# One DMA per raw Q, K, V chunk, and matmuls that read each block of 160 columns as two streams 80 columns apart

## The chip, the cores and the metric

The kernel runs on one core of one Trainium2 chip. The metric is the device time of one execution in microseconds (us). Before the change three runs gave 609.98, 607.99 and 611.25 us; their median is 609.98 us.

The engines of a core as the profile names them: PE multiplies matrices (PEld is its loading of the stationary operand), DVE and ACT work on vectors, POOL is the general engine, and SP here only issues transfers. SBUF is the on-chip memory with 128 partitions, PSUM the memory into which PE adds up its products. A matmul keeps one operand (128 x 128) stationary and streams the other, the moving operand, past it, column by column.

## The reference

With S = 2048 tokens, D = 640, F = 1536, H = 32 heads of 20:

```python
xn  = layernorm(x)
qkv = xn @ wqkv                     # (2048, 640) @ (640, 1920): queries, keys, values
idx = pos[:, None] - arange(8) * 2  # each token looks at 8 tokens, two apart, backwards
s   = softmax(q . k[idx] * scale) @ v[idx] @ wo        # masked where idx < 0
g   = silu(silu(xn @ w1) @ w2)      # (640, 1536), (1536, 640)
out = x + s * g
```

All values are float32.

## The kernel before

**Tiles.** The tokens are worked on in four groups of 512 (`NG = 4`): two halves of the sequence by two parities, since a window takes every second token. A group has `T = 4` tiles of 128 tokens. In each group the phase `qkv_phase` makes the queries, keys and values, then `ffn_phase` makes the two feed-forward products, with the product by `wo` of the group before in between; the last group's `wo` stands at the end (`wo_last`).

**Products in three parts.** Every float32 operand is split into a high part (rounded to the type fp32r) and a low part (the rest). A product is high x high + low x high + high x low: three matmuls (L881, L882, L883 for queries, keys and values, L1060 to L1062 for `w1`, L925 and L927 for `w2` and `wo`).

**The query, key and value phase.** It runs in four quarters (`NQ`), each with 8 heads = `CQ` = 160 columns of Q, of K and of V, 480 together. A quarter adds up over `DC` = 5 chunks of 128 rows of `wqkv`; for each chunk and each of 4 token tiles come three matmuls with the 480 columns as moving operand, so 60 matmuls in a quarter. ACT then copies the sums out of PSUM, K and V together by L633 and Q by L635, and SP moves rows of K and V between partitions (`halo`, L646). DVE makes the scores (L672, L675) and weighs the values (L714, L720).

**Weights.** Each chunk of weights passes through a ring of 7 SBUF tiles (`WR`, printed `w0` to `w6`). At its first use the raw chunk is loaded by `raw_load` (issued at L521) into a place lent by another tile (`pr`, `xr` or `gate`), ACT makes the high part (L557) and DVE or, for the first ten chunks, POOL the low part (L561); the two halves are then stored to memory (L566) and later loaded again by POOL (L548). Of Q, K and V 20 chunks are split, 8 of them twice, so `raw_load` brings 28 such chunks.

**Order of columns before.** A raw chunk of 480 columns is brought by two DMAs. It lies in SBUF as two halves of 240 columns: K and the first half of Q, then V and the second half of Q. The helper `two` makes the matmul read column m and column m + 240 in turn, so that in PSUM K and V alternate, and behind them the two halves of Q; `paired` reads every second column when ACT copies.

**Order of the work.** `Weave` records every operation with an assumed duration and an order of priority, plays the whole through and emits the instructions in the order of the starts that it assumes; PE's order is given by the program, the others' come out of that play. A DMA of SP counts with 0.62 us for each transfer of a raw chunk at the start and 0.45 later (`len(pairs)` is the number of transfers), one of ACT with 0.65. `LANES = 8` is the number of transfers of an engine that `Weave` lets be under way. In the first quarter (`first_quarter`, matmuls at L828) PE's order is a list written by hand (`FIRST`), since data are still arriving: the four token tiles of x are loaded one by one (L836, L583), get their statistics (L797, L798) and are normalised (L802), PE transposes them (L812), and ACT and DVE split them (L816, L817).

Of the kernel before, what the change touches and what calls it, by code (L numbers as in the profile page):

```python
# [10 lines left out]
AF = mybir.ActivationFunctionType  # L11
# [4 lines left out]
S, D, F, H, DH = 2048, 640, 1536, 32, 20  # L16
# [4 lines left out]
CQ = HQ * DH  # L21
# [3 lines left out]
HALO = W - 1  # L25
# [45 lines left out]
def two(ap, at, n, apart):  # L71

    a = [list(ap.ap[0]), [1, n // 2], [apart, 2]]
    return bass.AP(tensor=ap.tensor, offset=ap.offset + at, ap=a)


def paired(ps, h=2):

    return ps.rearrange("p (m h) -> p h m", h=h)


def halves_of(ap):
    return ap.rearrange("p (h m) -> p h m", h=2)


def tsl(t):
    return slice(t * P, (t + 1) * P)
# [218 lines left out]
def local_attention_silu_ffn(ctx: ExitStack, tc: tile.TileContext, x, wqkv, wo, w1, w2, out):  # L306
    nc = tc.nc
# [72 lines left out]
    def bank():  # L380
        i = take("acc", 6)
        return ACC[i], ("acc", i)
# [6 lines left out]
    mm = lambda n: n / 2400 + 0.0027  # L389
# [7 lines left out]
    def act(n, fn, reads, writes, prio, table=None, more=0.0, late=0.0, at=0.0, spans=()):  # L397
        return add("ACT", ac(n) + more, fn, reads, writes, prio, table=table, late=late, at=at, spans=spans)
# [64 lines left out]
    for u in units:  # L463
        n = seen[u] = seen.get(u, 0) + 1
# [6 lines left out]
    def width(i):  # L471
        return 3 * CQ if units[i][0] == "q" else D
# [8 lines left out]
    def raw_tile(k):  # L481


        if k < DC:
            return "pr", k
        if k < early:
            s = (k - DC) % 6
            return ("xr", s) if s < 2 else ("g", s - 2)
        return "xr", k % 3

    def raw_load(k):
        i = fresh[k]
# [12 lines left out]
        if u[0] == "q":  # L505
            _, q, c = u
            whole = wqkv[c * P:(c + 1) * P, :]
            to = halves_of(r)
            pairs.append((to[:, :, :CQ], whole[:, D:].rearrange("p (s m) -> p s m", s=2)[:, :, q * CQ:(q + 1) * CQ]))
            pairs.append((to[:, :, CQ:], halves_of(whole[:, q * CQ:(q + 1) * CQ])))  # L510
        elif u[0] == "w1":
            pairs.append((r.rearrange("p (c f) -> p c f", c=DC),
                          w1.rearrange("(c p) f -> p c f", p=P)[:, :, u[1] * P:(u[1] + 1) * P]))
        else:
            m = wo if u[0] == "wo" else w2
            pairs.append((r, m[u[1] * P:(u[1] + 1) * P, :]))
        by = nc.scalar if k in BY_ACT else nc.sync

        def go():
            for to, frm in pairs:  # L520
                by.dma_start(to, frm)  # L521
        if k in BY_ACT:
            add("ACT", 0.65 * len(pairs), go, [], kr, -1, nbytes=n * P * 4)
            return
        dma(go, [], kr, n * P * 4, 1 + k if k < 2 * DC else clock[0] + 5, (0.62 if k < 2 * DC else 0.45) * len(pairs))
# [51 lines left out]
    def w_done(n=1):  # L577
        for _ in range(n):
            w_load()
# [50 lines left out]

    def evac_qkv(g, q, t, ps, kp):
        kv, qq = KV[q], Q[q]
        act(2 * CQ, lambda: nc.scalar.activation(kv[:, :, HALO + t, :], paired(ps[:, :2 * CQ]), AF.Copy),  # L633
            [kp], [(k, q, t) for k in ("kv", "own", "val")], -1 if (g, q) in KEYS_FIRST else 0)
        act(CQ, lambda: nc.scalar.activation(halves_of(qq[:, t, :]), paired(ps[:, 2 * CQ:3 * CQ]), AF.Copy), [kp], [("q", q, t)], 0)  # L635

    def halo(g, q):
        h, par = groups[g]
# [139 lines left out]
    def first_quarter(i):  # L778

        ps, ws = {}, []  # L780
# [39 lines left out]
        def product(t, k, c):  # L820

            o, kp = ps[t]
            x, kx = (TL, "tl") if k == 1 else (TH, "th")
            wh, wl, kh, kl = ws[c]
            w, kw = (wl, kl) if k == 2 else (wh, kh)
            first, last = t not in given, given.get(t, 0) == 3 * DC - 1
            given[t] = given.get(t, 0) + 1
            pe(mm(3 * CQ), lambda: nc.tensor.matmul(  # L828
                o[:, :3 * CQ].rearrange("p (m h) -> p m h", h=2), x[i][:, c, tsl(t)], two(w, 0, 3 * CQ, 3 * CQ // 2),
                start=first, stop=last), [(kx, i, c, t), kw], [kp])  # L830

        given = {}
# [14 lines left out]
        for t in range(T):  # L847
            b, kp = bank()
# [15 lines left out]
    def qkv_phase(g, i, io):  # L864
        for q in range(NQ):
            if g == 0 and q == 0:
                ps = first_quarter(i)
            else:
                ps = [bank() for t in range(T)]
                for c in range(DC):  # L870
                    wh, wl, kh, kl = w_next("q", q, c)
                    for t in range(T):
                        o, kp = ps[t]

                        n = wh.shape[-1]

                        def unit(c=c, t=t, o=o, wh=wh, wl=wl, n=n):
                            o = o[:, :n].rearrange("p (m h) -> p m h", h=2)
                            hi, lo = TH[i][:, c, tsl(t)], TL[i][:, c, tsl(t)]
                            vh, vl = (two(w, 0, n, n // 2) for w in (wh, wl))  # L880
                            nc.tensor.matmul(o, hi, vh, start=c == 0, stop=False)  # L881
                            nc.tensor.matmul(o, lo, vh, start=False, stop=False)  # L882
                            nc.tensor.matmul(o, hi, vl, start=False, stop=c == DC - 1)  # L883
                        pe(3 * mm(n), unit, t_keys(i, [c], [t]) + [kh, kl], [kp])
# [287 lines left out]
```

## Time and profile before

| | before |
|---|---|
| median of three runs | 609.98 us |
| the profiled execution, its own time | 607.58 us |
| its span in the profile | 605.8 us |
| granted PE clock | 0.999 of full speed |
| PE busy, of the span | 596.8 us, 99% |
| DVE, ACT, POOL busy | 519.7, 222.1, 164.1 us |
| mean rate of all DMA | 265 GB/s |

The profile is of one execution. "Busy" of PE overlaps and its ends are modelled, so a matmul's cost is read from the distance between the starts of two that follow each other, in a timeline. A row of a timeline gives start and duration in us, the engine (SPq and ACTq are the queues from which transfers are issued), the line, operation, tile written and tiles read, how often, and in brackets the idle time before it with what ended it. In a table by stages a row gives the stretch, its length, each engine's busy time with the number of its instructions, the granted clock, the mean busy share of the 16 DMA engines and GB/s. The core's transfers by SP are in DMA queue q1.

### The profile page before, as it was taken

The numbers are of one execution on the slowest core, as the hardware profiler recorded it, in microseconds if no ns is written. First come the engines' busy times: TensorE is split into PE (matmuls) and PEld (weight loads), VectorE is DVE, ScalarE is ACT, GpSimd is POOL, SyncE is SP. The second block draws the span as 40 slices with busy tenths as digits, with TensorE's granted clock in tenths as the row PEclk, the third lists the DMA queues.
The fourth block names the chain that finished last, engine by engine and source line by source line (L and its number), as shares of the span: only waits on it lengthen the run. The fifth ranks groups of instructions, "written<-read, shape, count | busy, mean of one in ns | idle before, by whom it ended". The sixth has DMA issues, their size and how long they took to land.

```text
span 605.8 us, 9169 instructions
## 1 busy us (share of the span) xinstructions
PE 596.8 (99%) x3495; PEld 561.1 (93%) x3495; DVE 519.7 (86%) x505; ACT 222.1 (37%) x426; POOL 164.1 (27%) x229
## 2 busy tenths in 40 slices
PE   7999999999999999999999999999999999999997
PEld 6999989999999999999999999999999999999897
DVE  6498999989899998999979998999727999998534
ACT  5436465444535323343325421342512351314220
POOL 5800102233110153343221126533122133431100
PEclk9999999999999999999999999999999999999999
DMA  8999999977999999665699999866789997766742
GB/s 251 315 270 300 299 410 396 352 259 235 283 344 334 338 281 295 196 195 141 192 331 288 335 334 303 257 198 186 219 215 288 306 320 252 253 186 206 212 158 87
DMA packets 70151, 160.81 MB, mean 265 GB/s; under 512 B 13421, under 2 KB 34125, under 8 KB 70109
## 3 DMA queue, kind: packets, MB, share of 16 engines
q0 software_dynamic: 19296, 79.31, 43.5%
q1 hardware_dynamic: 50125, 80.52, 43.2%
q8 instruction: 27, 0.44, 0.3%
q10 hardware_dynamic: 688, 0.41, 0.2%
q14 instruction: 15, 0.12, 0.1%
HBM read 107.91 MB, written 34.16 MB: 235 GB/s over the span
## 4 chain that ended last, share of the span: by engine, by line
PE 91%; DMA 5%; DVE 2%; SPq 1%; issue 0%; ACT 0%; ACTq 0%; DVEq 0%
PE acc L925 22%; PE acc L927 14%; PE acc L881 9%; PE acc L883 9%; PE acc L882 9%; PE rot L1060 8%; PE rot L1062 8%; PE rot L1061 8%; PE rot L612 2%; PE acc L828 1%; DMA half_w<-w 1%; DMA gate<-in_B_w_dram 1%; DMA half_q<-w 1%; DMA pr<-in_A_wqkv_dram 1%; DMA xin<-in_A_x_dram 1%; SPq L521 1%
## 5 line engine op out<-in xcount | busy, mean ns | idle before, releaser
L881 PE MATMUL acc<-w,th 128*128 128x480 f32 x300 | 110.8, 369 | 0.0
L882 PE MATMUL acc<-w,tl 128*128 128x480 f32 x300 | 109.8, 366 | 0.0
L883 PE MATMUL acc<-w,th 128*128 128x480 f32 x300 | 109.8, 366 | 0.0
L925 PE MATMUL acc<-w,sh 128*128 128x384 f32 x384 | 109.1, 330 | 0.0
L672 DVE TENSOR_TENSOR pr<-q,kv 128x2560 f32<-128x2560 f32 x32 | 91.9, 2873 | 19.7 <-DMA kv<-kv 19.4
L927 PE MATMUL acc<-w,sh 128*128 128x256 f32 x384 | 104.7, 273 | 0.0
L1060 PE MATMUL rot<-th,w 128*128 128x512 f32 x240 | 92.3, 385 | 1.5 <-DVE tl L622 1.0
L714 DVE TENSOR_TENSOR pr<-q,kv 128x2560 f32<-128x2560 f32 x32 | 90.3, 2822 | 1.0
L1061 PE MATMUL rot<-tl,w 128*128 128x512 f32 x240 | 91.0, 379 | 0.0
L1062 PE MATMUL rot<-th,w 128*128 128x512 f32 x240 | 91.0, 379 | 0.0
L675 DVE TENSOR_REDUCE l<-pr 128x128 f32<-128x2560 f32 x32 | 89.7, 2802 | 0.3
L548 POOL DMA_DIRECT2D w<-half_w x72 | 38.9, 540 | 161.5 <-PE acc L927 54.0
L927 PEld LDWEIGHTS acc<-w,sh 128*128 128x128 f32 x384 | 73.7, 192 | 0.6
L925 PEld LDWEIGHTS acc<-w,sh 128*128 128x128 f32 x384 | 72.6, 189 | 0.6
L1073 ACT ACTIVATE sh<-rot 128x512 fp32r<-128x512 f32 x48 | 28.7, 598 | 112.8 <-PE rot L1062 112.7
L548 POOL DMA_DIRECT2D w<-half_q x52 | 27.8, 535 | 120.6 <-PE acc L883 71.5
L883 PEld LDWEIGHTS acc<-w,th 128*128 128x128 f32 x300 | 56.7, 189 | 4.0
L882 PEld LDWEIGHTS acc<-w,tl 128*128 128x128 f32 x300 | 56.7, 189 | 3.8
L881 PEld LDWEIGHTS acc<-w,th 128*128 128x128 f32 x300 | 56.7, 189 | 3.8
L925 PE MATMUL acc<-w,sl 128*128 128x384 f32 x192 | 55.9, 328 | 0.0
L1060 PEld LDWEIGHTS rot<-th,w 128*128 128x128 f32 x240 | 45.4, 189 | 7.9 <-DVE tl L622 1.2
L616 ACT ACTIVATE th<-rot 128x512 fp32r<-128x512 f32 x33 | 19.8, 600 | 88.8 <-PE rot L612 88.7
(101 smaller groups left out, 1084.0 us busy)
## 6 DMA issues: line engine op xcount, KB each, us to landing
w<-half_w POOLq DMA_DIRECT2D x72, 640.0 KB, 5.4
w<-half_q POOLq DMA_DIRECT2D x52, 480.0 KB, 4.7
half_w<-w SPq DMA_DIRECT2D x24, 640.0 KB
half_q<-w SPq DMA_DIRECT2D x20, 480.0 KB
kv<-kv SPq DMA_DIRECT2D x15, 560.0 KB
w<-half_wo POOLq DMA_DIRECT2D x10, 640.0 KB, 5.4
kv<-kv SPq DMA_DIRECT2D x15, 420.0 KB
gate<-in_B_w_dram SPq DMA_DIRECT2D x16, 320.0 KB
```

The source lines that it names most:

```text
L548: add("POOL", 1.0, lambda: nc.gpsimd.dma_start(both, src), [("half", u)], [kh, kl], due + 10, nbytes=2 * n * P * 4)
L672: dve(2560, lambda: nc.vector.tensor_tensor(out=PR, in0=win(qq[:, t:t + 2, :], W, 0), in1=win(kv[:, 0, t:t + 2, :], W, CQ), op=OP.mult), h ...
L675: dve(2560, lambda: nc.vector.tensor_reduce(out=l[:, t:t + 2].rearrange("p t w h -> p (t w h)"), in_=PR.rearrange("p t w (h d) -> p (t w h ...
L714: dve(2560, lambda: nc.vector.tensor_tensor(out=PR.rearrange("p t w (h d) -> p t (w h) d", d=DH), in0=e[:, t:t + 2].rearrange("p t w h -> ...
L881: nc.tensor.matmul(o, hi, vh, start=c == 0, stop=False)
L882: nc.tensor.matmul(o, lo, vh, start=False, stop=False)
L883: nc.tensor.matmul(o, hi, vl, start=False, stop=c == DC - 1)
L925: nc.tensor.matmul(a[t][0][:, :CA].rearrange("p (m h) -> p m h", h=2), st, col_a(w), start=first, stop=last)
L927: nc.tensor.matmul(b[t // 2][0][:, h * CB:(h + 1) * CB].rearrange("p (m h) -> p m h", h=2), st, col_b(w), start=first and h == 0, stop=las ...
L1060: nc.tensor.matmul(to, wh[:, cs], hi, start=c == 0, stop=False)
L1061: nc.tensor.matmul(to, wh[:, cs], lo, start=False, stop=False)
L1062: nc.tensor.matmul(to, wl[:, cs], hi, start=False, stop=c == DC - 1)
```

## The change

The raw chunk comes by one DMA of three runs of 160 columns a partition, and lies in SBUF as Q, K, V, in the order of the matrix. The helper `trio` replaces `two` for these chunks: the matmul reads, in each of the three blocks of 160 columns, column m and column m + 80 in turn. `trio_sums` names the same 480 PSUM columns as 3 x 80 x 2, which is one unbroken run as before. The copies out of PSUM (L633 and L635 before) take blocks 1 and 2 and block 0 and put the two halves of a block side by side. Nothing else in the program's text is changed; the ring, the split into high and low, the stored halves and the other matmuls (`two` with 320 and 256 columns between the streams) stay.

```diff
+def trio(w):
+
+    return bass.AP(tensor=w.tensor, offset=w.offset, ap=[list(w.ap[0]), [CQ, 3], [1, CQ // 2], [CQ // 2, 2]])
+
+
+def trio_sums(ps):
+    return ps[:, :3 * CQ].rearrange("p (k m h) -> p k m h", k=3, h=2)
@@ raw_load
-            to = halves_of(r)
-            pairs.append((to[:, :, :CQ], whole[:, D:].rearrange("p (s m) -> p s m", s=2)[:, :, q * CQ:(q + 1) * CQ]))
-            pairs.append((to[:, :, CQ:], halves_of(whole[:, q * CQ:(q + 1) * CQ])))
+            pairs.append((r.rearrange("p (k m) -> p k m", k=3), whole.rearrange("p (k m) -> p k m", k=3)[:, :, q * CQ:(q + 1) * CQ]))
@@ evac_qkv
-        act(2 * CQ, lambda: nc.scalar.activation(kv[:, :, HALO + t, :], paired(ps[:, :2 * CQ]), AF.Copy),
+        sums = trio_sums(ps).rearrange("p k m h -> p k h m")
+        act(2 * CQ, lambda: nc.scalar.activation(kv[:, :, HALO + t, :].rearrange("p k (h m) -> p k h m", h=2), sums[:, 1:], AF.Copy),
...
-        act(CQ, lambda: nc.scalar.activation(halves_of(qq[:, t, :]), paired(ps[:, 2 * CQ:3 * CQ]), AF.Copy), [kp], [("q", q, t)], 0)
+        act(CQ, lambda: nc.scalar.activation(halves_of(qq[:, t, :]), sums[:, 0], AF.Copy), [kp], [("q", q, t)], 0)
@@ product (first quarter)
-                o[:, :3 * CQ].rearrange("p (m h) -> p m h", h=2), x[i][:, c, tsl(t)], two(w, 0, 3 * CQ, 3 * CQ // 2),
+                trio_sums(o), x[i][:, c, tsl(t)], trio(w),
@@ qkv_phase
-                            o = o[:, :n].rearrange("p (m h) -> p m h", h=2)
...
-                            vh, vl = (two(w, 0, n, n // 2) for w in (wh, wl))
+                            vh, vl = trio(wh), trio(wl)
```

Since a chunk now counts as one transfer, `Weave` plays the program through with other durations, and the order of SP, DVE and ACT changes in the first three groups; PE's order is the same. Lines of the changed program stand 7 or 8 lower than before in these places (L521 is L528, L561 is L568).

SP at the very start (`xin` is the tile for x, `pr` and `xr` hold raw chunks), before:

```order
L836 DMA xin_105<-in_A_x_dram 128x320
L583 DMA xin_105<-in_A_x_dram 128x640
L521 DMA pr_102<-in_A_wqkv_dram 128x2x160
L521 DMA pr_102<-in_A_wqkv_dram 128x2x80
L521 DMA pr_102<-in_A_wqkv_dram 128x2x160
L521 DMA pr_102<-in_A_wqkv_dram 128x2x80
L521 DMA pr_102<-in_A_wqkv_dram 128x2x160
L521 DMA pr_102<-in_A_wqkv_dram 128x2x80
L521 DMA pr_102<-in_A_wqkv_dram 128x2x160
L521 DMA pr_102<-in_A_wqkv_dram 128x2x80
L583 DMA xin_105<-in_A_x_dram 128x640
L521 DMA xr0_107<-in_A_wqkv_dram 128x2x160
```

The same place after the change:

```order
L844 DMA xin_105<-in_A_x_dram 128x320
L590 DMA xin_105<-in_A_x_dram 128x640
L528 DMA pr_102<-in_A_wqkv_dram 128x3x160 x4
L590 DMA xin_105<-in_A_x_dram 128x640
L528 DMA xr0_107<-in_A_wqkv_dram 128x3x160
L528 DMA xr1_108<-in_A_wqkv_dram 128x3x160
L590 DMA xin_105<-in_A_x_dram 128x640
```

Eight issues between the second and the third token tile of x became four.

DVE in the first group, where the scores of quarter 0 and the low parts of the chunks of quarters 2 and 3 are made (`w5` and `w6` are the third and fourth chunk of quarter 2, `w0` the fifth, `w1` the first of quarter 3), before:

```order
L672 TENSOR_TENSOR pr_102<-q0_97,kv0_93 128x2560
L561 TENSOR_TENSOR w5_80<-xr1_108,w5_80 128x480
L561 TENSOR_TENSOR w6_81<-gate_106,w6_81 128x480
L561 TENSOR_TENSOR w1_76<-gate_106,w1_76 128x480
L675 TENSOR_REDUCE l0_103<-pr_102 128x128
L561 TENSOR_TENSOR w0_75<-gate_106,w0_75 128x480
```

The same place after the change:

```order
L680 TENSOR_TENSOR pr_102<-q0_97,kv0_93 128x2560
L568 TENSOR_TENSOR w5_80<-xr1_108,w5_80 128x480
L683 TENSOR_REDUCE l0_103<-pr_102 128x128
L568 TENSOR_TENSOR w6_81<-gate_106,w6_81 128x480
L568 TENSOR_TENSOR w0_75<-gate_106,w0_75 128x480
L568 TENSOR_TENSOR w1_76<-gate_106,w1_76 128x480
```

The long reduction of the scores moved ahead of the low part of `w6`.

More of the change, by code (lines that the diff above doesn't have):

```diff
@@ L873, in qkv_phase, with unit @@
                         o, kp = ps[t]
-                        n = wh.shape[-1]
-                        def unit(c=c, t=t, o=o, wh=wh, wl=wl, n=n):
-                            o = o[:, :n].rearrange("p (m h) -> p m h", h=2)
+                        def unit(c=c, t=t, o=trio_sums(o), wh=wh, wl=wl):
                             hi, lo = TH[i][:, c, tsl(t)], TL[i][:, c, tsl(t)]
-                            vh, vl = (two(w, 0, n, n // 2) for w in (wh, wl))
+                            vh, vl = trio(wh), trio(wl)
                             nc.tensor.matmul(o, hi, vh, start=c == 0, stop=False)
@@ L883, in unit @@
                             nc.tensor.matmul(o, hi, vl, start=False, stop=c == DC - 1)
-                        pe(3 * mm(n), unit, t_keys(i, [c], [t]) + [kh, kl], [kp])
+                        pe(3 * mm(3 * CQ), unit, t_keys(i, [c], [t]) + [kh, kl], [kp])
                     w_done()
```

## The prediction

> **What bounds it.** I read the page's busy times and its chain first, then a table by stages, then timelines of the one stage in which PE idles.
>
> ```profile
> PE 596.8 (99%) x3495; PEld 561.1 (93%) x3495; DVE 519.7 (86%) x505; ACT 222.1 (37%) x426; POOL 164.1 (27%) x229
> PE 91%; DMA 5%; DVE 2%; SPq 1%; issue 0%; ACT 0%; ACTq 0%; DVEq 0%
> ...
> 7.39:22.82 15.43, 14.71 (x78) 12.39 (x77) 9.39 (x27) 8.50 (x23) 10.30 (x11) 1.00 1.00 297
> 22.82:59.30 36.48, 36.48 (x182) 34.04 (x181) 30.01 (x35) 17.02 (x38) 7.05 (x6) 1.00 1.00 293
> 59.30:135.00 75.70, 75.21 (x449) 70.03 (x448) 72.52 (x68) 37.98 (x67) 15.18 (x17) 1.00 0.97 340
> 135.00:602.00 467.00, 465.70 (x2766) 440.33 (x2764) 403.69 (x358) 155.69 (x295) 128.25 (x189) 1.00 0.85 252
> ```
>
> PE is busy for 99% of the span, and 91% of the chain that ends last is PE. The stages are the first quarter (from its first product to its last), the other three quarters of group 0, its feed-forward phase, and all the rest. Length less PE's busy time is idle time: 0.72, 0.00, 0.49 and 1.30 us, 2.5 us together. So only two things can move the end by much: the time that a matmul takes, or a new wait of PE. DMA is the second thing to see: its share is 1.00 from 7 to 59 us, so a transfer there waits for bytes ahead of it.
>
> **The matmuls.** The change touches those with 480 columns.
>
> ```profile
> L881 PE MATMUL acc<-w,th 128*128 128x480 f32 x300 | 110.8, 369 | 0.0
> L828 PE MATMUL acc<-w,th 128*128 128x480 f32 x40 | 11.5, 382 | 0.0
> L828 PE MATMUL acc<-w,tl 128*128 128x480 f32 x20 | 6.7, 385 | 0.0
> ...
> 22.82 0.37 PE L881 MATMUL acc<-w,th 128*128 128x480 f32 x1
> 59.27 0.38 PE L1060 MATMUL rot<-th,w 128*128 128x512 f32 x1
> ...
> 104.18 0.38 PE L1062 MATMUL rot<-th,w 128*128 128x512 f32 x1
> 105.91 0.38 PE L1061 MATMUL rot<-tl,w 128*128 128x512 f32 x1
> ```
>
> There are 15 quarters of 60 (L881 to L883, 300 each) and 60 in the first quarter: 960. The 0.37 is a modelled length; the cost is the distance of starts. From 22.82 to 59.27 stand three quarters, 180 matmuls: 36.45 / 180 = 0.2025 us each, 0.422 ns a column, and 960 x 0.2025 = 194.4 us in all. The matmuls for `w1` read their 512 columns as two streams 256 apart: eight starts in 105.91 - 104.18 = 1.73 us are 0.216 each, again 0.422 ns a column. So 240 columns (960 bytes) or 256 (1024 bytes) between the streams cost the same, and 80 columns (320 bytes) with two jumps between blocks is the one new thing. The output is the same unbroken run of PSUM. I take no change: a gain is excluded because two different distances give one price, so the distance is not what limits them; a loss is bounded below.
>
> **The start.** Here the change removes transfers.
>
> ```profile
> 1.22 0.44 SPq L583 DMA_DIRECT2D xin<-in_A_x_dram  x1
> 1.70 5.13 SPq L521 DMA_DIRECT2D pr<-in_A_wqkv_dram  x8
> 6.88 0.47 SPq L583 DMA_DIRECT2D xin<-in_A_x_dram  x1
> ...
> SPq L521 <- DMA pr<-in_A_wqkv_dram: 0.7, 1, 0.7
> SPq L521 <- DMA xin<-in_A_x_dram: 0.6, 1, 0.6
> ...
> 11.13 0.89 DVE L797 BATCH_NORM_STATS2 st<-xin 128x6 f32<-128x320 f32 x2 [1.14 <-DMA xin<-in_A_x_dram]
> ...
> 11.40 1.18 PE L828 MATMUL acc<-w,th 128*128 128x480 f32 x5
> 13.29 0.44 PE L812 MATMUL rot<-ident,xin 128*128 128x128 f32 x2 [0.71 <-DVE xin L802]
> ...
> GB/s 0 0 2 66 304 371 402 320 337 311 314 243 212 250 193 342 307 263 192 259 320 324 324 294 299 295 372 360 230 181 192 226 303 420 380 372 432 355 353 421
> ```
>
> The rows are SP's queue, its waits in the first 10 us, DVE, PE, and the DMA rate. SP issues x's third tile at 6.88, behind eight issues that take 5.13 us, 0.7 + 0.6 = 1.3 us of it waits for the landing of earlier transfers. DVE gets that tile at 11.13, and PE waits for what DVE makes of it: the five products from 11.40 would be through their starts at 11.40 + 5 x 0.2025 = 12.41, and the transposes of the third tile begin at 13.29. That is 0.88 us lost.
>
> After the change four issues stand there. At 5.13 / 8 = 0.64 each they end at 4.3, so x's third tile is queued 2.6 us earlier. It cannot land 2.6 earlier, because the bytes ahead of it are the same. The rates (slices of 0.6 us of the first 24 us) are 314 GB/s at 6.0 to 6.6 us, then 243, 212, 250 and 193 while too little is queued: 224.5 on average. With the queue filled, (314 - 224.5) x 2.4 us = 0.215 MB would move in that time too, worth 0.215 / 314 GB/s = 0.68 us.
>
> ```profile
> DMA packets 1557, 0.70 MB, mean 270 GB/s; under 512 B 828, under 2 KB 1557, under 8 KB 1557
> q1 hardware_dynamic: 1557, 0.70, 110.4%
> ...
> DMA packets 446, 1.10 MB, mean 275 GB/s; under 512 B 35, under 2 KB 85, under 8 KB 446
> q1 hardware_dynamic: 446, 1.10, 91.7%
> ```
>
> The second part is packets: a chunk had 256 of 640 bytes and 256 of 320, now 384 of 640. The first pair of rows covers 5.4 to 8.0 us, the second 17 to 21. Share x 16 engines x stretch / packets gives 29.5 ns at a mean of 450 bytes (0.70 MB / 1557), and 132 ns at 2466: about 0.051 ns a byte and 7 ns a packet. 128 packets less are 128 x 7 / 16 = 0.05 us a chunk, 0.25 us for the five ahead of x's third tile. Together it lands 0.9 us earlier, and the wait of 0.88 would be gone; if the queue gains nothing it stays. I take 0.8, near the upper end, since SP's order and the dip in the rates both point there.
>
> The Trainium skill, "DMA: Bandwidth & Descriptors", Specifications, says that transfers under 512 bytes fall below line rate since they are read and modified. If a packet of 320 bytes cost as much as one of 640 (7 + 0.051 x 640 = 40 ns), the five chunks would save 5 x 128 x 40 / 16 = 1.6 us, but PE's wait caps the gain at the same 0.88; by the rows here the small packets cost less than that.
>
> **The second wait.** One wait of PE in the feed-forward phase comes from late raw weights.
>
> ```profile
> 62.86 6.87 DMA gate<-in_B_w_dram
> 69.75 8.37 DMA half_w<-w
> 78.14 0.74 ACT w L557
> ...
> 79.03 0.38 PE L1062 MATMUL rot<-th,w 128*128 128x512 f32 x1
> 79.90 0.48 PE L1060 MATMUL rot<-th,w 128*128 128x512 f32 x1 [0.49 <-ACT xin L618]
> ```
>
> A start due at 79.03 + 0.216 comes at 79.90: 0.66 us lost behind ACT, which in the chain of waits stands behind transfers. By then 20 raw chunks have come, 20 x 0.05 = 1.0 us of DMA time less, and ACT's order changes there. Between nothing and 0.66 I take 0.3.
>
> **The copies and the rest.** The copies keep their sizes (320 and 160 elements, read from PSUM at every second column as before), so I cost them at nothing.
>
> ```profile
> L633 ACT ACTIVATE kv<-acc 128x320 f32<-128x320 f32 x64 | 28.2, 440 | 45.2 <-PE acc L883 34.0 <-issue 9.6 <-PE acc L828 1.6
> L635 ACT ACTIVATE q<-acc 128x160 f32<-128x160 f32 x64 | 19.5, 306 | 0.0
> ```
>
> What hides them is ACT's idle time and the six PSUM banks: a quarter takes four, so the next one runs two tiles (6 matmuls, 1.2 us) before it needs a bank of the last. Without that cover a quarter would wait 0.44 + 0.31 = 0.75 us, 12 us in 16 quarters. The other halves of weights, POOL's loads and the low parts have unchanged sizes.
>
> **Sum.** 607.58 - 0.8 - 0.3 = 606.5 us for an execution like the profiled one, of which 605.8 is the span. The median of the runs shown is 2.4 us above that execution, so against it the forecast is 609.98 - 1.1 = 608.9 us.
>
> **Rivals.** *The transfers are hidden anyway.* DMA is at a share of 1.00, and if x's third tile comes when it came, PE's waits stay and the time is 609.98. The dip to 193 GB/s speaks against it.
>
> *The new streams are slower.* Two streams 320 bytes apart, or the two jumps, cost each of the 960 matmuls something; every ns is 0.96 us, and from 3.2 + 1.1 = 4.3 ns on (2% of 0.2025 us) the kernel is slower by over 0.5%. The nearest row of a moving operand read without two streams is the float32 transpose:
>
> ```profile
> 103.31 0.60 PE L612 MATMUL rot<-ident,xin 128*128 128x128 f32 x4
> 103.66 0.46 PE L1060 MATMUL rot<-th,w 128*128 128x512 f32 x1
> ```
>
> Four in 0.35 us are 0.68 ns a column, which would make 480 columns 0.328 us and the kernel 121 us longer, 730 us. That is the far end; it is another type and another mode, and the rows of 0.422 ns at two distances speak for no loss, so I give this rival little, with about 10 us (620) as its likelier size. The Trainium skill, "SBUF — State Buffer", Specifications (TRN2), states 16-byte lines that need two hits each for full bandwidth, which speaks against reading in turns; yet the kernel before already changes lines at every column and runs at 0.422 ns, so this trace does not bear it out.
>
> *The new order makes PE wait.* DVE now does the long reduction before the low part of `w6`.
>
> ```profile
> 35.12 2.82 DVE L672 TENSOR_TENSOR pr<-q,kv 128x2560 f32<-128x2560 f32 x1
> 38.43 0.65 DVE L561 TENSOR_TENSOR w<-gate,w 128x480 fp32r<-128x480 f32 x1
> 40.12 2.81 DVE L675 TENSOR_REDUCE l<-pr 128x128 f32<-128x2560 f32 x1
> ```
>
> Before, that low part was ready at 39.1. Its first reader is the third matmul of quarter 2's fourth chunk: 22.82 + 12.15 + 3 x 2.43 + 0.4 = 42.7, less the 0.8 won, 41.9. In the new order it is ready at 35.12 + 2.8 + 0.6 + 2.8 + 0.6 = 41.9. So it is just in time, and PE loses what L672 begins later than 35.12, up to a reduction of 2.8. Two such places would cost 5.6 - 1.1 = 4.5 us: 614.5 us. For it speaks that DVE is 86% busy; against it that DVE had slack of 3 us here.
>
> **Numbers.** The forecast (PE's waits at the start and at 79 us shorter, no new cost) gets 0.55, the hidden transfers 0.20, the new order 0.13, slower streams 0.12. A measurement of this kernel can tell about 0.5%, 3.05 us, from no change. All of PE's idle time after 7.39 us is 2.5 us, so faster by more than that needs scatter between runs (607.99 to 611.25) on top: 0.07. Slower by more: half of the new order, most of the streams, a little scatter: 0.20. The same: 0.73. The forecast's own range is 607 to 611; the range down to 605.8 and up to 614.5 takes in scatter, the one reduction too many and streams slower by 5 ns, and leaves out the rest of the streams.
>
> **What would show it.** Right: in the changed profile 180 matmuls of three quarters again take 36.45 us; the third x tile is issued near 4 us, DVE starts on it near 10.2, and the transposes after the fifth product follow without idle time; PE's idle time in the first quarter is near zero. Wrong: a distance over 0.207 us between the starts of L881 to L883's successors, or rows of PE waiting for a low part `w` between 35 and 135 us.

## The result, and the profile after

| | before | after |
|---|---|---|
| median | 609.84 us | 605.62 us |
| lowest and highest | 607.56 to 611.25 us | 605.24 to 607.39 us |
| the profiled execution | 607.58 us | 605.28 us |
| its span | 605.8 us | 603.5 us |

The changed kernel takes 0.9933 of the time before, 95% interval 0.9911 to 0.9956: 4.2 us or 0.67% less. It was forecast at 608.9 us with a range down to 605.8; it is faster than that, by more than the trace of before had to give in idle time of PE. A second series (`after_again` below) gave 0.9928 (0.9906 to 0.9950). One execution of all those on record (621.32 us, of `stores_by_act`) was slow as a whole and is left out of the figures.

The page of the changed kernel, busy times and chain:

```profile
PE 597.0 (99%) x3495; PEld 562.0 (93%) x3495; DVE 518.4 (86%) x505; ACT 222.2 (37%) x426; POOL 165.7 (27%) x229
PE 98%; DVE 1%; DMA 1%; ACT 0%; issue 0%
```

The table by stages (first quarter, other three quarters of group 0, its feed-forward phase):

```profile
7.17:21.52 14.35, 14.35 (x79) 12.52 (x77) 10.25 (x29) 8.41 (x23) 10.26 (x11) 1.00 1.06 359
21.52:57.97 36.45, 36.45 (x182) 34.02 (x180) 31.88 (x37) 18.43 (x43) 6.97 (x6) 1.00 1.04 316
57.97:135.00 77.03, 77.03 (x464) 72.20 (x463) 72.95 (x69) 40.31 (x67) 15.71 (x17) 1.00 0.93 330
```

PE's share hardly moved, but the chain did: DMA had 5% of it and now has 1%. The first three stages have no idle time of PE at all. The first quarter moves its bytes at 359 GB/s instead of 297.

The beginning of the second quarter and of the feed-forward phase on PE:

```profile
21.52 0.37 PE L886 MATMUL acc<-w,th 128*128 128x480 f32 x1
57.97 0.38 PE L1065 MATMUL rot<-th,w 128*128 128x512 f32 x1
```

The 180 matmuls between them take 36.45 us, 0.2025 each, to the hundredth what they took before.

The start, from SP's, DVE's and PE's timelines:

```profile
1.67 2.68 SPq L528 DMA_DIRECT2D pr<-in_A_wqkv_dram  x4
4.39 0.61 SPq L590 DMA_DIRECT2D xin<-in_A_x_dram  x1
...
9.85 0.89 DVE L805 BATCH_NORM_STATS2 st<-xin 128x6 f32<-128x320 f32 x2
...
11.20 1.18 PE L836 MATMUL acc<-w,th 128*128 128x480 f32 x5
12.21 0.38 PE L820 MATMUL rot<-ident,xin 128*128 128x128 f32 x2
```

x's third tile is issued at 4.39 us in place of 6.88. DVE starts on it at 9.85 in place of 11.13, without a wait, and PE goes from its five products (11.20 + 5 x 0.2025 = 12.21) to the transposes without one.

How the 2.3 us between the two profiled executions come together: the first product starts 0.22 us earlier (7.17, before 7.39); the first quarter loses 1.10 us less; the feed-forward phase 0.75 us less; what follows the last matmul is 0.23 us shorter, which nothing here explains. "Lost" means here and below the distance of two starts on PE less the usual one (0.2025 us for 480 columns, 0.216 for 512), added up over a stage. That is 2.3 of the 4.2 us that the medians differ by. The other 1.9 us are the experiments' first question.

### The profile page after: what moved, and what is told of

It is laid out like the page before. It is cut to its first block, busy times and chain, and to the rows that moved or that the text cites. A ratio compares the mean times of both kernels' runs of the same rounds, so it can differ in the third digit from the quotient of the medians.

```text
span 603.5 us, 9128 instructions
## 1 busy us (share of the span) xinstructions
PE 597.0 (99%) x3495; PEld 562.0 (93%) x3495; DVE 518.4 (86%) x505; ACT 222.2 (37%) x426; POOL 165.7 (27%) x229
## 3 DMA queue, kind: packets, MB, share of 16 engines
q0 software_dynamic: 19296, 79.31, 43.4%
q1 hardware_dynamic: 46237, 80.52, 43.0%
## 4 chain that ended last, share of the span: by engine, by line
PE 98%; DVE 1%; DMA 1%; ACT 0%; issue 0%
PE acc L930 22%; PE acc L932 15%; PE acc L886 10%; PE acc L887 10%; PE acc L888 10%; PE rot L1065 9%; PE rot L1067 9%; PE rot L1066 9%; PE rot L619 2%; PE acc L836 2%; DMA xin<-in_A_x_dram 1%; PE rot L820 0%; PE rot L1048 0%; DVE st L805 0%; DVE tl L629 0%; ACT th L623 0%
## 5 line engine op out<-in xcount | busy, mean ns | idle before, releaser
L932 PE MATMUL acc<-w,sl 128*128 128x256 f32 x192 | 52.3, 273 | 0.0
```

The source lines that it names most:

```text
L932: nc.tensor.matmul(b[t // 2][0][:, h * CB:(h + 1) * CB].rearrange("p (m h) -> p m h", h=2), st, col_b(w), start=first and h == 0, stop=las ...
```

## The experiments

Each series is compared with the kernel before, run beside it on the same chip (its medians there: 608.99 to 610.80 us); the ratio, not the difference of two medians, is the fair comparison. The last three columns are PE's lost time in the profiled execution, in us: in the first quarter (8 to 25 us of the span), in the rest of the quarters of group 0 (to 60), and in its feed-forward phase (to 135).

| kernel | median, us | ratio, 95% interval | 8-25 | 25-60 | 60-135 |
|---|---|---|---|---|---|
| before (profile of the forecast) | 609.84 | 1 | 1.37 | 0 | 0.75 |
| `before_again` | 609.94 | 1.0001, 0.9980 to 1.0021 | 1.33 | 0 | 2.92 |
| after | 605.62 | 0.9933, 0.9911 to 0.9956 | 0.27 | 0 | 0 |
| `after_again` | 605.35 | 0.9928, 0.9906 to 0.9950 | 0.24 | 0 | 0 |
| `one_dma_old_order` | 605.74 | 0.9937, 0.9915 to 0.9958 | 0.29 | 0 | 0 |
| `two_dma_new_order` | 610.84 | 1.0022, 1.0001 to 1.0043 | 1.27 | 1.29 | 2.41 |
| `two_dma_new_layout` | 609.95 | 0.9993, 0.9966 to 1.0019 | 1.08 | 0 | 2.50 |
| `one_dma_first5` | 608.70 | 0.9975, 0.9956 to 0.9994 | 0.27 | 0 | 1.40 |
| `one_dma_from6` | 607.26 | 0.9953, 0.9933 to 0.9973 | 0.79 | 0 | 0 |
| `three_dmas` | 616.35 | 1.0104, 1.0075 to 1.0133 | 3.22 | 3.53 | 4.87 |
| `contiguous_read` | 619.35 | 1.0153, 1.0126 to 1.0181 | - | - | - |
| `second_by_act` | 612.81 | 1.0053, 1.0033 to 1.0073 | 6.70 | 0.10 | 0 |
| `stores_by_act` | 609.65 | 0.9999, 0.9981 to 1.0016 | 2.00 | 1.52 | 0 |
| `small_by_sp` | 611.65 | 1.0014, 0.9988 to 1.0041 | 0.32 | 1.01 | 7.47 |
| `small_by_act` | 611.64 | 1.0013, 0.9990 to 1.0036 | 5.57 | 0 | 0 |
| `small10_by_sp` | 608.07 | 0.9978, 0.9956 to 1.0000 | 0.27 | 0 | 4.70 |
| `small10_by_pool` | 605.88 | 0.9944, 0.9923 to 0.9965 | 0.26 | 0.25 | 0 |

### Which part of the change it is

The change does three things: fewer transfers, other packets and streams, another order on DVE and ACT. Each was taken apart. `one_dma_old_order` lets the planner go on counting two transfers, so that DVE and POOL keep the order of before:

```diff
-            add("ACT", 0.65 * len(pairs), go, [], kr, -1, nbytes=n * P * 4)
+            add("ACT", 0.65 * (2 if u[0] == "q" else 1), go, [], kr, -1, nbytes=n * P * 4)
...
-        dma(go, [], kr, n * P * 4, 1 + k if k < 2 * DC else clock[0] + 5, (0.62 if k < 2 * DC else 0.45) * len(pairs))
+        dma(go, [], kr, n * P * 4, 1 + k if k < 2 * DC else clock[0] + 5, (0.62 if k < 2 * DC else 0.45) * (2 if u[0] == "q" else 1))
```

> The changed kernel (one DMA a chunk, streams 80 apart), but its planner still counts two transfers a chunk, so that DVE and POOL keep the old order word for word. Theory 'transfers' (the gain comes from fewer transfers being under way, at the start above all): as fast as the changed kernel, about 605.6 us, PE's 0.88 us wait for the third x tile gone. Theory 'order' (the gain comes from what the planner moved): about 609 us, with only the wait at the start gone.

605.74 us, as the changed kernel: the new order has no part in the gain. `two_dma_new_order` is the converse, the kernel before with 1 in place of `len(pairs)` in these two lines.

> The kernel before (two DMAs a chunk, streams 240 apart), but its planner counts one transfer a chunk, so that DVE and POOL have the changed kernel's order word for word. Theory 'order': about 606.5 us. Theory 'transfers': about 609.8 us or more, with PE still waiting 0.9 us for the third x tile.

610.84 us, 0.22% slower than before, the interval just clear of 1. PE, in quarter 2:

```profile
36.13 0.37 PE L883 MATMUL acc<-w,th 128*128 128x480 f32 x1
37.34 0.47 PE L881 MATMUL acc<-w,th 128*128 128x480 f32 x1 [0.85 <-ACT q L635]
```

With two transfers in fact and one in the plan, PE loses 1.01 us there, behind ACT's copies, which leave PSUM later; with one in fact the same order on DVE loses nothing. The rival "the new order makes PE wait" expected a loss of up to 2.8 us in quarter 2 (counted from 0), behind the low part of `w6`. A loss does come at the start of that quarter, but it is 1.01 us and behind a copy by ACT, so that mechanism is not what these rows show.

`two_dma_new_layout` has the layout, the streams and the copies of the changed kernel and only runs of 640 bytes, but two transfers a chunk (K and V, then Q):

```diff
-            pairs.append((r.rearrange("p (k m) -> p k m", k=3), whole.rearrange("p (k m) -> p k m", k=3)[:, :, q * CQ:(q + 1) * CQ]))
+            to, frm = r.rearrange("p (k m) -> p k m", k=3), whole.rearrange("p (k m) -> p k m", k=3)[:, :, q * CQ:(q + 1) * CQ]
+            pairs.append((to[:, 1:], frm[:, 1:]))
+            pairs.append((to[:, 0], frm[:, 0]))
```

> The changed kernel's columns and streams, but each chunk brought by two DMAs (K with V, then Q) of 640-byte runs only, planner and order as before the change. It has the number of transfers of before without their 320-byte packets. Theory 'number of transfers': about 609.8 us as before, wait for the third x tile 0.9 us. Theory 'packets' (the small packets were what cost): about 606 us, the wait gone.

609.95 us, no gain. Against `one_dma_old_order` it differs in nothing but the number of transfers, and that is worth 4.2 us (3.4 by the two ratios). Neither the packets of 320 bytes nor the streams have a share that shows within this interval (0.9966 to 1.0019).

The kernel before was run again beside these:

> The kernel before, unchanged, for another profile: its runs lie at 607.6 to 608.0 and at 609.5 to 611.3 us, and the profile used for the prediction was one at 607.58. Ratio 1.000. If this profile is one near 611, the 3 us more show where: 'start' says before 25 us, as longer waits for the first transfers; 'later transfers' says between 25 and 140 us, where DMA is at a share of 1.00; 'clock' says nowhere in particular, with the distance of matmul starts over 0.2025 us throughout.

Its median is that of before, but this profiled execution took 609.79 us. PE's timeline at 79 us:

```profile
79.07 0.38 PE L1062 MATMUL rot<-th,w 128*128 128x512 f32 x1
82.11 0.48 PE L1060 MATMUL rot<-th,w 128*128 128x512 f32 x1 [2.66 <-ACT xin L618]
```

The chain of waits that leads there:

```profile
64.09 6.96 DMA gate<-in_B_w_dram
71.06 9.27 DMA half_w<-w
80.35 0.74 ACT w L557
```

It is the same wait as in the forecast's profile and behind the same transfers, but 2.82 us are lost to it instead of 0.66. That is the 2.2 us by which the two executions differ: this wait changes from execution to execution, and the profile that the forecast used shows a small one.

### How much comes from which chunks

`one_dma_first5` has one transfer for the first quarter's five chunks and two for the later ones, with `to` and `frm` as above and the order of before; `one_dma_from6` is the converse, with `k >= DC`.

```diff
+            pairs += [(to, frm)] if k < DC else [(to[:, 1:], frm[:, 1:]), (to[:, 0], frm[:, 0])]
```

> The changed kernel with the order of DVE and POOL as before, and one transfer only for the five chunks of the first quarter; each later chunk comes by two transfers (320 and 160 columns, all packets 640 bytes). Theory 'two places' (the change gains about 1.3 us at the start, and the rest of its 4.2 us because the later chunks leave fewer transfers in SP's queue, so that the raw weights for w1 and w2 are in time): PE's wait near 12 us is gone, a loss of 0.7 to 2.8 us between 64 and 82 us is there, median about 608.2 us (0.9978 of the kernel before). Rival 'all from the start' (SP is ahead from the first chunks on, and stays so): no loss at 64 to 82 us, median 605.7.

> The converse: two transfers for each of the first quarter's five chunks, one for each later chunk. Theory 'two places': the wait of PE near 12 us is there (0.7 to 0.9 us), none at 64 to 82 us, median about 606.9 us (0.9957). Rival 'all from the start': the loss at 64 to 82 us comes back (0.7 to 2.8 us), median about 609.5.

608.70 and 607.26 us. By the ratios that is 1.5 and 2.9 us less than before (0.9975 and 0.9953 of 609.62, the median of before in this series), together 4.4 us; by the medians themselves it is 0.9 and 2.4, together 3.3. Each ratio is uncertain by about 1.2 us, so the two parts make up the gain of about 4 us as far as can be told. The waits follow: with the first five alone the one at 12 us is gone and one of 1.30 us stays near 79 us. With the later ones alone nothing is lost from 60 to 135 us, and the first quarter loses 0.79 us; but only 0.20 of that is at the third tile's transposes, less than the 0.7 to 0.9 expected there. The rival, that SP is ahead from the first chunks on and stays so, falls. So about two thirds of the gain come from chunks which PE multiplies by long before the place where it waits: what they delay is what stands behind them in SP's queue.

`three_dmas` doubles the suspected cost, with Q, K and V of a chunk apart:

```diff
+            pairs += [(to[:, b], frm[:, b]) for b in range(3)]
```

> The changed kernel with the order of DVE and POOL as before, and three transfers for each raw chunk (Q, K and V apart, 128 packets of 640 bytes each); bytes, packets and layout are the same as with one. Theory 'number of transfers': one more transfer costs at least what the second did, 4.2 us in the median: 613 to 620 us, the wait near 12 us doubles to 1.5 us or more, and the loss at 64 to 82 us is 3 us or more. Rival 'it is the pair, a fixed cost that is paid once a chunk is divided': 609.5 us, waits as with two.

616.35 us. The steps are 4.2 us for the second transfer and 6.4 for the third (3.4 and 6.8 by the ratios), where the bytes, their packets and the layout are the same as with one. PE's waits (total, times, longest):

```profile
PE rot L1066 <- ACT xin L626: 1.9, 1, 1.9
PE acc L889 <- DVE w L569: 1.6, 2, 0.9
PE acc L887 <- ACT q L644: 1.3, 2, 1.1
```

The second row is new: now PE also waits for low parts of Q, K, V chunks (L569), at 44.5 and 50.4 us in quarter 2 (counted from 0). Every stage of group 0 is late.

### Why a transfer more costs time

Two things could do it: SP, or the DMA engines that carry out the transfer. The built programs' lists of SP, with the semaphores that each transfer waits for around x's third tile, before and then changed:

```
8 L521 DMA pr<-in_A_wqkv_dram 128x2x80 [waits DMAHW2_49]
9 L521 DMA pr<-in_A_wqkv_dram 128x2x160 [waits DMAHW3_49]
10 L521 DMA pr<-in_A_wqkv_dram 128x2x80 [waits DMAHW4_49]
11 L583 DMA xin<-in_A_x_dram 128x640 [waits DMAHW5_49]
```

```
3 L528 DMA pr<-in_A_wqkv_dram 128x3x160 x4
4 L590 DMA xin<-in_A_x_dram 128x640 [waits DMAHW0_49]
5 L528 DMA xr_107<-in_A_wqkv_dram 128x3x160 [waits DMAHW1_49]
```

In these programs SP and ACT share eight semaphores in turn. Every transfer takes the next one and first waits until the transfer that had it, eight issues earlier, has landed. A transfer more thus costs SP its issue (0.43 to 0.62 us in the median of these profiles) and one of eight places, whatever its size. When the first raw chunk of `w1` is issued is the measure of how late SP is (form, count, shortest/median/longest issue in ns, first and last start in us); before, `before_again`, after:

```profile
L521 SPq DMA_DIRECT2D gate<-in_B_w_dram x16: 332/386/1332, 48.0 to 117.1; - x16
```

```profile
L521 SPq DMA_DIRECT2D gate<-in_B_w_dram x16: 327/386/1208, 49.2 to 119.3; - x16
```

```profile
L528 SPq DMA_DIRECT2D gate<-in_B_w_dram x16: 332/400/2230, 42.5 to 111.2; - x16
```

48.0 and 49.2 us with two, 42.5 with one. SP's longest waits from 20 to 65 us, before and after:

```profile
SPq L521 <- DMA kv<-kv: 2.7, 2, 1.7
SPq L646 <- ACT w L557: 2.0, 3, 1.3
```

```profile
SPq L528 <- DVE l L683: 3.0, 2, 1.9
SPq L654 <- ACT w L564: 2.8, 2, 1.7
SPq L590 <- PE acc L836: 1.7, 1, 1.7
```

In all SP stands still for 8.4 us of this stretch before the change, half of it for landings (of the shifts of K and V above all), and for 12.7 us after, nearly all of it for engines that free a place. What it waits for is no sure sign: in `one_dma_old_order`, as fast as the changed kernel, 6.0 of 12.4 us are waits for landings. How long it waits at all is a better one. In the eight profiles that lose time from 60 to 135 us it is 7.1 to 10.4 us, in the nine others 11.4 to 17.0: there SP has caught up with the work.

Two experiments took transfers away from SP and left each chunk its two: `second_by_act` gives ACT the second transfer of a chunk from the sixth chunk on, `stores_by_act` the stores of the split halves.

```diff
-            for to, frm in pairs:
-                by.dma_start(to, frm)
+            for n, (to, frm) in enumerate(pairs):
+                (nc.scalar if n and k >= DC else by).dma_start(to, frm)
```

```diff
-            dma(lambda: nc.sync.dma_start(kept, both.bitcast(F32)), [kh, kl], [("half", u)], 2 * n * P * 4, due + 25)
+            q = nc.scalar if u[0] == "q" else nc.sync
+            dma(lambda: q.dma_start(kept, both.bitcast(F32)), [kh, kl], [("half", u)], 2 * n * P * 4, due + 25)
```

> The changed kernel's layout and reading, two transfers a chunk as in two_dma_new_layout (same number, bytes, packets, and the same order on DVE and POOL), but from the sixth chunk on the second transfer of a chunk is issued by ACT instead of SP. Theory 'SP's queue is what is late' (the time that SP needs to issue, and its wait for the landing of earlier ones): the loss at 64 to 82 us is gone, the wait of PE near 12 us stays (0.7 to 0.9 us), the raw weights are issued from about 42 us on as in the changed kernel, median about 607.2 us as with one_dma_from6. Rival 'a transfer more costs the DMA engines something, whoever issues it': loss at 64 to 82 us of 0.7 to 2.8 us, median about 609.7. A third way: ACT is held up by issuing, and PE waits for a high part or a copy out of PSUM in quarters 2 to 4; then over 610.

> As two_dma_new_layout (two transfers a chunk, all by SP but the first chunk's), but the stores of the split halves of Q, K, V chunks are issued by ACT instead of SP; nothing about the raw chunks is changed. Theory 'SP's queue is what is late': the loss at 64 to 82 us is gone or under 0.5 us although every chunk still takes two transfers, the wait near 12 us stays, median 607 to 607.8 us. Rival 'it is the raw chunks' own second transfer': loss as with two, median about 609.7 us.

In both, nothing is lost from 60 to 135 us. But 6.7 and 3.5 us are lost before, so PE comes there later, and the medians are 612.81 and 609.65. The raw weights are issued from 49.8 and 49.1 us on, not from 42. The theory's wait from 60 to 135 us came out, its times did not: the third way took place, ACT was held up. These two are no clean proof.

`after_again` was the control beside them:

> The changed kernel once more. Both theories: 605.7 us (605.2 to 607.4), PE loses nothing between 25 and 135 us.

Next, load was added to the changed kernel instead: behind each raw chunk from the sixth on a copy of 2560 bytes from memory to memory, no part of the computation. `small_by_sp` has SP issue it, `small_by_act` ACT (`nc.scalar`).

```diff
+            if u[0] == "q" and k >= DC:
+                small = dram.tile([1, D], F32, name=f"small_{k}")
+                nc.sync.dma_start(small, wo[k:k + 1, :])
```

> The changed kernel (order of DVE and POOL as before), one transfer for each raw chunk; behind each raw chunk of Q, K, V from the sixth on SP issues one small transfer more, 2560 bytes from memory to memory, which nobody waits for and which waits for nothing (16 packets of 160 bytes). Theory 'SP's queue is what is late' (23 issues more of about 0.5 us each, 15 of them before 60 us): the loss at 64 to 82 us comes back, 0.7 to 2.8 us, the raw weights are issued from about 47 us on instead of 42, median about 608.7 us as with one_dma_first5. Rival 'the raw chunk's own second landing, or its bytes': no loss there, 605.7 us. If only the landings of larger transfers hold SP up, something between, near 606.5.

> The same small transfers, issued by ACT in place of SP. Theory 'SP's queue is what is late': no loss at 64 to 82 us, raw weights from about 42 us on, median 605.7 us, or up to 606.5 if ACT's 23 issues of about 0.6 us make something late. Rival 'a transfer more costs the DMA engines something, whoever issues it': as small_by_sp.

`small_by_sp` took 611.65 us, 1.0014 of before where `one_dma_old_order` takes 0.9937: 23 tiny copies cost 4.7 us, more than the later chunks' second transfers (2.9), and their bytes cannot be the reason. The loss at 64 to 82 us is back, and larger than expected (4.25 us in two waits). The control failed. `small_by_act` took 611.64 us, with its loss at another place, in ACT's timeline:

```profile
5.75 0.56 ACTq L531 DMA_DIRECT2D small<-in_A_wo_dram  x1
...
10.91 0.50 ACTq L531 DMA_DIRECT2D small<-in_A_wo_dram  x1
11.46 0.30 ACT L606 ACTIVATE sd<-mv,epst 128x1 f32<-128x1 f32 x1 [3.88 <-DMA xr<-in_A_wqkv_dram]
```

The second small copy stood before a square root (L606) that PE's next transposes need. It was waiting for its semaphore, that is for the landing of a raw chunk, ACT stood behind it for 3.88 us, and PE lost 3.9 us at 8.35. The lists of ACT here and of POOL in the next kernel show why:

```
10 L531 DMA small_243<-in_A_wo_dram 16x40 [waits DMAHW2_49]
```

```
34 L531 DMA small_482<-in_A_wo_dram 16x40 [waits DMASW0_49]
```

ACT's transfers take the same eight places as SP's; POOL's have semaphores of their own. The last pair issues the small copies from the eleventh chunk on, 18 of them, once by SP and once by POOL (`k >= 2 * DC`, and `nc.gpsimd` in the second).

> The changed kernel (order of DVE and POOL as before), one transfer a raw chunk, and behind each raw chunk from the eleventh on one small transfer by SP (2560 bytes, 18 of them, 10 before 60 us) that nobody waits for. Every transfer of SP and ACT takes the next of eight semaphores and waits for the landing of the transfer that had it, so a small one uses up a place, and about 0.5 us of SP. Theory 'SP's queue and its eight places': the loss at 64 to 82 us is there, 0.5 to 3 us, none before 25 us; median 607 to 610 us. Rival 'only the first ten chunks' transfers matter': 605.7 us.

> The same 18 small transfers at the same places of the program, but issued by POOL, which has eight semaphores of its own: the DMA engines get the same transfers, SP neither the issues nor the waits. Theory 'SP's queue and its eight places': no loss at 64 to 82 us, raw weights issued from about 42 us on, 605.7 us, up to 606.3 if POOL's low parts come later. Rival 'a further transfer costs in the DMA engines, whoever issues it': as small10_by_sp.

608.07 and 605.88 us. The same copies cost 2.2 us behind SP and nothing that can be measured behind POOL. They are not quite alike on the DMA side: the 576 packets of the copies are in queue q1 with SP's other transfers in the first kernel (46237 packets become 46813) and in q0 with POOL's in the second (19296 become 19872). The first raw chunk of `w1`, SP's kernel and then POOL's:

```profile
L528 SPq DMA_DIRECT2D gate<-in_B_w_dram x16: 327/383/1207, 46.6 to 119.2; - x16
```

```profile
L528 SPq DMA_DIRECT2D gate<-in_B_w_dram x16: 328/414/1317, 43.1 to 115.2; - x16
```

PE's waits in the same order:

```profile
PE rot L1068 <- ACT xin L628: 2.9, 1, 2.9
```

```profile
PE rot L795 <- POOL ident masks.py:199: 1.4, 1, 1.4
PE rot L1068 <- DVE tl L632: 1.0, 1, 1.0
```

Behind POOL only the wait for the identity at the very start and the one at 571 us are left, both also in the changed kernel. The delay is there before the DMA engines get the raw weights: SP issues them late. So it is SP's queue, and not the transfers' own work.

Issuing, or the wait for a place? The number of places was not varied, but the traces tell how SP spends its time up to the first raw chunk of `w1`: the number of its transfers until then, the sum of the durations of their issues, and the rest, which is waiting of either kind.

| kernel | first chunk of `w1`, us | transfers before it | issuing, us | rest, us |
|---|---|---|---|---|
| `one_dma_old_order` | 41.7 | 42 | 29.2 | 11.7 |
| before | 48.0 | 62 | 36.2 | 11.1 |
| `two_dma_new_layout` | 47.6 | 62 | 35.4 | 11.5 |
| `three_dmas` | 56.2 | 82 | 44.7 | 10.8 |
| `small10_by_sp` | 46.6 | 53 | 37.3 | 8.5 |
| `small10_by_pool` | 43.1 | 42 | 30.9 | 11.4 |

The waiting does not grow with the number of transfers; the issuing does, and it accounts for the whole delay. With two transfers a chunk the waits for landings do rise, from 2.4 us in `one_dma_old_order` to 5.3 and 5.8 in the next two rows, but the waits for engines fall by at least as much. In `small10_by_sp` only 0.5 us of the rest is waiting for landings, and the loss is there all the same. So for the later chunks the price is the issue itself. At the very start the places count too: in the first 10 us SP waits 1.3 us for landings before the change and not at all after it. What an issue may wait for within its own duration, the profile does not show.

### What the streams are worth

`contiguous_read` lets the matmul read its 480 moving columns one after the other.

```diff
 def trio(w):
-    return bass.AP(tensor=w.tensor, offset=w.offset, ap=[list(w.ap[0]), [CQ, 3], [1, CQ // 2], [CQ // 2, 2]])
+    return w[:, :3 * CQ]
 def trio_sums(ps):
-    return ps[:, :3 * CQ].rearrange("p (k m h) -> p k m h", k=3, h=2)
+    return ps[:, :3 * CQ]
```

> The changed kernel with the order of DVE and POOL as before, but the matmuls of Q, K and V read their 480 moving columns one after the other instead of as two streams 80 columns apart; ACT's copies take plain runs. Theory 'the way of reading costs nothing between 80 and 256 columns apart, but a plain read is dearer' by the row of the float32 transposes (0.68 ns a column in place of 0.422): 960 matmuls of 0.328 us in place of 0.2025, about 726 us. Rival 'the way of reading costs nothing at all': starts 0.2025 us apart, 605.7 us.

619.35 us: neither. The three quarters on PE:

```profile
22.23 0.38 PE L886 MATMUL acc<-w,th 128*128 128x480 f32 x1
...
61.23 0.38 PE L1065 MATMUL rot<-th,w 128*128 128x512 f32 x1
```

39.00 us for 180 matmuls are 0.2167 each, 0.451 ns a column in place of 0.422. 960 x 0.0142 = 13.6 us, and the kernel is 13.6 us above `one_dma_old_order`. A plain read costs 7%, not the 62% of the float32 transposes; two streams 80, 240 or 256 columns apart are alike.

No run is faster than the changed kernel. In it PE loses nothing from 25 to 135 us; what is left are about 3 us before the first products, 1.2 us at 571 us (the same wait for a low part, here L629, in every profile) and 4.2 us after the last matmul, and the change touches none of them.

## Why the prediction was wrong

**The step that failed is the second wait.** The mechanism was the right one (raw weights late behind the transfers of SP), but its size was read from one execution: "between nothing and 0.66 I take 0.3". It is 0.66 us there and 2.82 in the next profile of the same kernel; over all runs the later chunks' transfers are worth 2.9 us (`one_dma_from6`, by its ratio). The bound drawn from it, that all of PE's idle time is 2.5 us and faster by more than 0.5% needs scatter, failed with it: a kernel 99% busy in one profile can be 2 us less so in the next. That the median of the runs stood 2.4 us above the profiled execution was in the forecast as an offset, and was the hint that waits were missing in that profile.

Not all of the scatter of before is this wait alone. In the five series of experiments that kernel ran 120 times. In 34 of these runs the mean granted clock of PE is 0.997 or less, and their median is 612.0 us; in the other 86 it is 609.1. None of the changed kernel's 15 runs lies under 0.998. Without the 34, the median of all 120 would be 609.1 instead of 609.6 us, so about half a microsecond of the gain comes with the clock. The last section shows a long wait that lowers the clock; that this is what happened in those 34 runs is likely but not shown, since none of them was profiled.

**The cause of the second wait was half seen.** It was costed as DMA time of packets, 0.05 us a chunk and 1.0 us for 20. `two_dma_new_layout` has none of the packets of 320 bytes and gains nothing (0.9993, 0.9966 to 1.0019). What counts is the number of transfers ahead on SP, which the prediction had used for x's third tile and not for the weights: 20 issues fewer before the first raw chunk of `w1`, 7 us of SP's time (`one_dma_old_order` against before).

**The start was right, and somewhat too small.** The tile was issued "near 4 us" (4.39) and the wait of 0.88 us is gone, as forecast. DVE starts on it 1.28 us earlier where 0.9 was worked out. Of that, 0.25 was for packets, and this part is not borne out: without small packets `two_dma_new_layout` still loses 0.72 us at this place, the two profiles of before 0.88 and 0.68. The first quarter loses 1.10 us less (0.8 was taken) and begins 0.22 us earlier, which was not foreseen; over all runs the first five chunks are worth 1.5 us, by the ratio.

**The matmuls were right to the hundredth:** 36.45 us for 180. The rival of slower streams falls. For its far end, 730 us, it took the row of the float32 transposes as a plain read; `contiguous_read`, with a plain read in these matmuls, takes 619.35 us, so that row was no measure for them. The Trainium skill, "SBUF — State Buffer", Specifications (TRN2), asks for two hits a 16-byte line; here the read in turns, which leaves a line at each column, takes 0.422 ns and the plain one 0.451, so this measurement goes against the rule.

**The copies and the order** cost nothing, as forecast (the copies take 440 and 305 ns, before 440 and 306), though the order only because the transfers are fewer (`two_dma_new_order` loses 1.01 us in quarter 2). *The transfers are hidden anyway* falls with the start.

**The forecast as a whole:** the sign was right for the profiled execution (606.5 forecast, 605.28 measured), but 1.1 us was taken off the median, where by the ratios 1.5 and 2.9 us went.

The Trainium skill, "DMA: Bandwidth & Descriptors", Specifications, says that transfers under 512 bytes fall below line rate. By this rule the 320-byte runs of before would have cost something. The packets themselves agree: in the first 24 us of the trace of before, those of 320 bytes take 21.2 ns each on average and those of 640 bytes 34.9, which is 0.066 against 0.055 ns a byte. In the kernel's time it does not show, since `two_dma_new_layout` without them is not faster.

## What to carry to other kernels

Count the transfers of a queue, not only their bytes: each one, however small, takes its issue out of the queue's time (about half a microsecond here), and the price is paid by whatever stands late in that queue, here the raw weights of the next phase. How much the queue stands still is a sign of how much room it has; what it stands still for is not. And a wait that depends on DMA must be sized from several executions, since one profile may show the smallest.

## What was not expected of the hardware

A longer wait of PE is paid twice. In `small10_by_sp` PE stands 2.89 us; its timeline:

```profile
77.67 0.38 PE L1070 MATMUL rot<-th,w 128*128 128x512 f32 x1
80.94 0.80 PE L1068 MATMUL rot<-th,w 128*128 128x512 f32 x1 [2.89 <-ACT xin L628]
81.53 0.63 PE L1069 MATMUL rot<-tl,w 128*128 128x512 f32 x1
...
83.66 0.60 PE L1068 MATMUL rot<-th,w 128*128 128x512 f32 x1
84.09 0.39 PE L1069 MATMUL rot<-tl,w 128*128 128x512 f32 x1
84.32 0.38 PE L1070 MATMUL rot<-th,w 128*128 128x512 f32 x1
```

From 81.53 to 84.09 the starts are 2.56 / 6 = 0.427 us apart, twice the 0.216 of a matmul of 512 columns, and then 0.23 and 0.216 again: half speed for about 3 us, 1.6 us lost on top of 3.05. The table by stages gives the granted clock in the third figure from the end:

```profile
79.00:82.00 3.00, 1.06 (x3) 0.88 (x4) 2.58 (x3) 2.82 (x6) 0.00 (x0) 0.78 1.04 413
82.00:90.00 8.00, 8.00 (x45) 7.34 (x44) 7.97 (x11) 4.84 (x8) 0.00 (x0) 0.87 1.03 410
```

At half clock these are (0.22 x 3 + 0.13 x 8) / 0.5 = 3.4 us. In `small_by_sp`, after 2.7 us of idle time at 80.31, it lasts to 89 us. After the wait of 2.66 us in `before_again` the distances are 0.216 from the second matmul on. The Trainium skill, "TensorE: Matmul & The Clock Gate", Part 1 (the clock gate), says that PE falls to half its clock after an idle window of about 3.4 us; the traces agree on the half, but here 2.89 and 2.7 us of idle time were enough.

A loss of 1.4 to 2.0 us at 486 to 490 us, far from the change, stands in the profiled executions of `one_dma_first5` and `stores_by_act` and in none of before and after. Its cause is open.
